# Values and gates of the last 64 tokens in plain float32, in two 64-column tiles side by side

## The chip, the cores and the metric

The kernel runs on one core of a Trainium2 chip. The metric is the device time of one execution in microseconds (us). The core has five engines that each run their own instructions in a fixed order and wait for each other by semaphores: PE (TensorE, matrix products), DVE (VectorE), ACT (ScalarE), POOL (GpSimd) and SP (SyncE, which here issues most of the transfers, the DMAs). Instructions are put in order when the kernel is built.

## The reference

Three stages follow one another: linear attention with a normalised output, a channel mixing stage, and an attention with four experts of which each token takes two. The change concerns the third stage. For each of 8 batches with 576 tokens of 512 features (here `x`, the output of the stage before):

```python
logits = x @ w_gate                      # 4 experts
topk = np.argpartition(-logits, K, axis=-1)[..., :K]     # K = 2
...
w = np.exp(sel)
w /= w.sum(-1, keepdims=True) + 1e-09
for e in range(E):
    q = x @ wq[e]                        # 64 columns each
    k = x @ wk[e]
    v = x @ wv[e]
    scores = scale * (q @ k.transpose(0, 2, 1))
    scores = np.where(causal, -1000000000.0, scores)
    ...
    a = np.exp(scores)
    a /= a.sum(-1, keepdims=True) + 1e-09
    ye = a @ v @ wo[e]
    # out += (gate weight of e, for tokens that chose e) * ye
```

`x` is the product of two arrays that the stage before leaves in memory, `x2d` and `sgd` (a gate).

## The kernel before

`phase_a` and `phase_v` compute the first two stages, `phase2` the experts. Most products are not done in plain float32 but from two parts: a value is split (`split`, L70 to L72) into a rounded part (`...h`, made by ACT) and the rest (`...l`, made by DVE or POOL), and `mm3` (L74 to L78) issues three matmuls for each block of 128 rows of the contraction. The contraction over 512 features has four blocks (KD), so one product of this kind has 12 matmuls. In the trace their lines are L76, L77 and L78.

The weights of `phase2` are loaded and split by `weights2` and its `load_w` during `phase_v`. The value weights of four experts (4 x 64 columns) and the gate weights (4 columns) lie side by side, 260 columns, as `wgh` and `wgl`. The unsplit weights pass through a staging tile `wst` with two buffers.

In `phase2` the 576 tokens of a batch lie in five chunks: four of 128 and a last one of 64. They are also cut into halves [0, 256) and [256, 576).

- `prep(b, hf)` loads a half of the two arrays (tiles `x2in` and `gin`, L779, issued by SP), multiplies them on POOL (L786), and splits the product into `x2h` (ACT, L787) and `x2l` (POOL, L788). `x2in` has two buffers, so a half of the next batch takes the buffer of the same half of this batch.
- `qk_group` makes queries or keys of a pair of experts for a half: 12 matmuls that move 256 or 320 columns. For a second half it also copies the last 64 queries into the block-diagonal tile `bd` (POOL, L821).
- `v_group(b, c)` makes values and gates of a chunk: 12 matmuls that move 260 columns, with the tokens as the stationary side, and a copy to `vs` (DVE, L831). For the last chunk (c = 4) it multiplies the last 128 tokens and copies only rows 64 to 127; rows 0 to 63 of that chunk of `vs` are zeroed once. Then `gate` (DVE, one exponential on ACT) turns the logits of the whole batch into gate weights `wg` and `wl`.
- `scores` computes scores of a chunk of queries for a pair of experts (matmuls of 64 x 128 tiles, L902), or for the last chunk of both experts at once from `bd` (L887). `expo` takes the exponential (ACT, L914), `norm` multiplies it by the inverse sum and the gate weight (POOL, L931), `transp` transposes it (PE, L951) four steps later, `attnv` multiplies it by the values in plain float32, with the two experts of a pair in two tiles of 64 columns (L978), and `wo_group` applies the output weights; its result goes out by a DMA of SP (L1005).

Scores of the last chunk for the first pair need a probability tile `pr` of 576 columns, of which the last transpose takes 128 columns in two blocks.

A batch has 18 steps (`seq`). Lists (`fill_q`, `fill_o`, `fill_n`, spread over the steps) say which group is issued at which step: the key, value and gate groups of the next batch run during this batch, and `v_group(b, 4)` is the last of them. The scheduler of the build may still move an instruction against others on its engine by its own estimate of when its data is there. On PE, `v_group(b, 4)` ends up between `v_group(b, 3)` and the first scores of batch b.

## Time and profile before

| | us |
|---|---|
| median of 3 runs (978.44 to 979.56) | 978.5 |
| the profiled execution | 979.24 |
| its span in the trace | 977.5 |
| PE busy in the span | 944.1 (97%) |
| DVE busy | 635.1 (65%) |
| ACT busy | 538.2 (55%) |
| POOL busy | 382.5 (39%) |

The profile shows one execution. The span runs from the first to the last recorded instruction, so the whole execution is 1.74 us longer than it. Shares are an average over the three stages. In `phase2`, which fills the span from about 600 us on, one batch takes 46.1 us. In a row of the timeline, "x12" is a run of twelve like instructions, the first figure is when the run starts and the second how long it lasts until its last end; the ends of matmuls are modelled, so the distance from start to start says more than the duration of one. A plain float32 matmul leaves two records.

### The profile page before, as it was taken

To read this page: it belongs to the slowest core of one execution; us is meant where nothing else is said; L and a number is where in the kernel's file an instruction comes from. 1 tells how busy PE (TensorE), PEld (TensorE's weight loads), DVE (VectorE), ACT (ScalarE), POOL (GpSimd) and SP (SyncE) were. 2 spreads that over 40 slices of the span, in tenths; PEclk is the share of its full clock that TensorE was granted. 3 is DMA by queue.
4 is the path that set the end of the run, shared out by engine and by line. 5 is a ranking of instruction groups with operands and counts; after the bars stand their busy time and mean duration, and the time that the engine had idled before them with its cause. 6 is when DMAs were issued, how large, how long until landed. Compare 5 with 4: busy or idle time off the path is not lost.

```text
span 977.5 us, 20974 instructions
## 1 busy us (share of the span) xinstructions
PE 944.1 (97%) x7912; PEld 866.8 (89%) x7912; DVE 635.1 (65%) x1535; ACT 538.2 (55%) x1320; POOL 382.5 (39%) x510
## 2 busy tenths in 40 slices
PE   5779999999999999999999999999999999999998
PEld 2668899999999999999999999888988888888977
DVE  4897675867595855458888873666556556556553
ACT  4664766656565665445454544546364646455554
POOL 0035052424252512632222225757373736364331
PEclk9789999999999999999999999999999999999999
DMA  9752637363736222766454545223131404020102
GB/s 340 239 164 92 224 107 240 107 222 99 233 111 210 95 80 92 214 196 195 155 157 159 157 135 186 79 77 103 44 120 28 121 26 146 2 98 1 50 13 85
DMA packets 81108, 127.19 MB, mean 130 GB/s; under 512 B 6512, under 2 KB 65392, under 8 KB 81008
## 3 DMA queue, kind: packets, MB, share of 16 engines
q1 hardware_dynamic: 71360, 112.36, 35.7%
q10 hardware_dynamic: 9648, 13.51, 4.2%
q8 instruction: 62, 1.02, 0.5%
q14 instruction: 38, 0.31, 0.1%
HBM read 78.66 MB, written 47.19 MB: 129 GB/s over the span
## 4 chain that ended last, share of the span: by engine, by line
PE 82%; DVE 7%; ACT 5%; DMA 3%; issue 2%; POOL 1%; ACTq 0%; SPq 0%; POOLq 0%; DVEq 0%
PE acc L76 16%; PE acc L77 16%; PE acc L78 15%; PE qa L676 7%; PE acc L978 5%; PE qd L676 4%; PE pt L951 4%; PE acc L676 4%; PE s L902 3%; PE acc L296 2%; PE s L887 1%; PE po L312 1%; PE acc L66 1%; ACT pr L914 1%; DMA kkd<-ksq 1%
## 5 line engine op out<-in xcount | busy, mean ns | idle before, releaser
L433 POOL TENSOR_TENSOR ksq<-rl 128x288 f32<-128x288 f32 x128 | 101.9, 803 | 150.1 <-ACT rl L431 144.9
L77 PE MATMUL acc<-mixl,wkh 128*128 128x288 f32 x512 | 154.1, 302 | 0.4 <-DVE mixl L66 0.4
L76 PE MATMUL acc<-mixh,wkh 128*128 128x288 f32 x512 | 151.1, 299 | 3.4 <-ACT mixh L405 2.8
L78 PE MATMUL acc<-mixh,wkl 128*128 128x288 f32 x512 | 151.2, 296 | 0.0
L914 ACT ACTIVATE pr<-pr,nm 128x256 f32<-128x256 f32 (+4 forms) x144 | 83.5, 581 | 72.1 <-DVE nm L868 71.3
L931 POOL TENSOR_SCALAR pr<-pr,rc,wg 128x512 f32<-128x512 f32 (+3 forms) x128 | 76.3, 609 | 72.5 <-DVE wg L861 54.2
L76 PEld LDWEIGHTS acc<-mixh,wkh 128*128 128x128 f32 x512 | 96.4, 190 | 4.6 <-ACT mixh L405 3.3
L77 PEld LDWEIGHTS acc<-mixl,wkh 128*128 128x128 f32 x512 | 97.0, 189 | 2.4 <-DVE mixl L66 0.6
L78 PEld LDWEIGHTS acc<-mixh,wkl 128*128 128x128 f32 x512 | 97.3, 190 | 0.0
L399 DVE TENSOR_TENSOR mixl<-xm,mixh 128x288 fp32r<-128x288 f32 x116 | 58.3, 538 | 51.7 <-ACT mixh L405 51.7
L431 ACT ACTIVATE rl<-acc 128x288 f32<-128x288 f32 x128 | 51.7, 406 | 71.0 <-PE acc L78 52.6
L868 DVE CUSTOM_DVE_ANT_0 pr<-s,mask 128x256 f32<-128x256 f32 (+4 forms) x144 | 66.9, 481 | 21.6 <-PE pt L951 16.9
L76 PE MATMUL acc<-mixh,wrh 128*128 128x288 f32 x240 | 74.6, 311 | 0.9 <-ACT sg L66 0.9
L404 DVE SCALAR_TENSOR_TENSOR xm<-xT,pars,xm 128x288 f32<-128x288 f32 x116 | 68.9, 623 | 5.1 <-ACT xm L396 5.0
L396 ACT ACTIVATE xm<-xT,nus 128x288 f32<-128x288 f32 x120 | 61.0, 533 | 18.7 <-DVE mixl L399 8.8
L78 PE MATMUL acc<-mixh,wrl 128*128 128x288 f32 x240 | 71.0, 296 | 0.0
L77 PE MATMUL acc<-mixl,wrh 128*128 128x288 f32 x240 | 70.4, 293 | 0.0
L76 PE MATMUL acc<-x2h,wqh 128*128 128x256 f32 (+1 forms) x224 | 69.5, 310 | 0.0
L72 DVE TENSOR_TENSOR kk<-tv,kk 128x1152 fp32r<-128x1152 f32 x32 | 51.4, 1607 | 27.2 <-ACT kk L71 27.1
L77 PE MATMUL acc<-x2l,wqh 128*128 128x256 f32 (+1 forms) x224 | 66.1, 295 | 0.0
L78 PE MATMUL acc<-x2h,wql 128*128 128x256 f32 (+1 forms) x224 | 66.1, 295 | 0.0
L951 PE MATMUL pt<-ident,pr 128*128 128x128 f32 x400 | 63.4, 277 | 0.6
(252 smaller groups left out, 2732.4 us busy)
## 6 DMA issues: line engine op xcount, KB each, us to landing
kkd<-ksq SPq DMA_DIRECT2D x128, 144.0 KB, 1.8
kin<-kkd SPq DMA_DIRECT2D x32, 576.0 KB, 4.1
kvt<-in_kv SPq DMA_DIRECT2D x24, 512.0 KB, 5.7
qt<-in_qT SPq DMA_DIRECT2D x16, 576.0 KB, 6.8
x2d<-vo SPq DMA_DIRECT2D x16, 576.0 KB, 3.7
sgd<-sg ACTq DMA_DIRECT2D x56, 144.0 KB, 3.2
out<-ob SPq DMA_DIRECT2D x28, 288.0 KB, 2.3
x2in<-x2d SPq DMA_DIRECT2D x7, 640.0 KB, 5.2
```

Source lines behind the costliest of these rows:

```text
L76: ten.matmul(ps, wh(i), xh(i), start=(i == 0), stop=False)
L77: ten.matmul(ps, wh(i), xl(i), start=False, stop=False)
L78: ten.matmul(ps, wl(i), xh(i), start=False, stop=(i == n - 1))
L396: act.activation(xs[p], xT[:, p, h * HS:(h + 1) * HS], AF.Copy, scale=nu[:, p:p + 1])
L399: vec.tensor_sub(xl[:, p, :], xs[p], xh[:, p, :].bitcast(F32))
L404: vec.scalar_tensor_tensor(xs[p], xT[:, p, cols(h)], mu[:, p:p + 1], xs[p], op0=ALU.mult, op1=ALU.add)
L433: nc.gpsimd.tensor_mul(sq, rl, rl)
L676: nc.tensor.matmul(q[:, :HS], a[:, i, ms_], c[:, i, :], start=(start and i == 0 and n == 0), stop=(stop and i == KH - 1 and n == 2), skip_ ...
L868: nc.vector.tensor_tensor_reduce(out=pr[:R, k0:k0 + kn], in0=s[:R, :kn], in1=mk, scale=1.0, scalar=lo, op0=ALU.add, op1=ALU.min, accum_out ...
L914: nc.scalar.activation(pr[:, :L], pr[:, :L], AF.Exp, bias=nm, scale=-1.0, accum_out=sms[b, p, j][:, e2:e2 + 1])
L931: nc.gpsimd.tensor_scalar(pr[:, :L], pr[:, :L], rc[:, r:r + 1], wg, op0=ALU.mult, op1=ALU.mult)
L951: nc.tensor.transpose(pt[:, (i - i0) * P:(i - i0 + 1) * P], pr[:, k1 - P:k1], ident)
```

## The change

`load_w` can be given the tile to load into, and the value and gate weights are loaded into a new tile `wg_raw` that stays. They are still split for the other chunks. For the last chunk, `v_group` takes the 64 tokens unsplit as the stationary side, from `xf`, and `wg_raw` as the moving side, in plain float32: for each of the four blocks one matmul of 128 columns (experts 0 and 1) whose result lies in rows 0 to 63, and one of 132 columns (experts 2 and 3, and the gates) whose result lies in rows 64 to 127. Two copies bring them to `vs`. Which rows of `vs` are zeroed changes with this, and the last chunk of the first pair takes a tile `wide` of its own that is 64 columns longer, zero there, so that the last transpose reads 128 columns that match the new rows. For batch 0, `xf` is a small tile that two more ACT copies fill at the end of `phase_v`; for the others it is `x2in` itself.

```diff
-        def load_w(wh, wl, w, kt, f, scaled=0):
-            st = w2.tile([P, DM], F32, name="wst", bufs=2)
+        wg_raw = W["wg_raw"] = w2.tile([P, KD, NV + E], F32, name="wg_raw")
+
+        def load_w(wh, wl, w, kt, f, scaled=0, st=None):
+            if st is None:
+                st = w2.tile([P, DM], F32, name="wst", bufs=2)
...
-            load_w(wgh, wgl, w_vg, i, NV + E)
+            load_w(wgh, wgl, w_vg, i, NV + E, st=wg_raw[:, i, :])
...
+                        if n > 2:
+                            act.activation(W["xf"][:, 2 * n - 6:2 * n - 4, :], x[:, :, x.shape[2] - MN:], AF.Copy)
...
+                xf[b] = x2[:, :, :w]
...
+            wide = sb.tile([P, S + P - MN], F32, name="wide", bufs=1)
+            nc.gpsimd.memset(wide[:, S:], 0.0)
+            xf = {0: W["xf"]}
...
-                    nc.gpsimd.memset(st_[b]["vs"][:P - MN, NC - 1, :], 0.0)
+                    nc.gpsimd.memset(st_[b]["vs"][MN:, NC - 1, :VC], 0.0)
+                    nc.gpsimd.memset(st_[b]["vs"][:P - MN, NC - 1, VC:], 0.0)
...
-                nc.vector.tensor_copy(t["vs"][P - n:, c, :], acc[P - n:, :NV + E])
-                if c == NC - 1:
+                if c < NC - 1:
+                    mm3(acc[:, :NV + E], lambda i: xh[:, i, a:a + P], lambda i: xl[:, i, a:a + P], lambda i: wgh[:, i, :], lambda i: wgl[:, i, :], KD)
+                    nc.vector.tensor_copy(t["vs"][:, c, :], acc[:, :NV + E])
+                else:
+                    parts = [(slice(0, MN), slice(0, VC)), (slice(P - MN, P), slice(VC, NV + E))]
+                    for i in range(KD):
+                        for rs, cs in parts:
+                            nc.tensor.matmul(acc[rs, :cs.stop - cs.start], xf[b][:, i, -MN:], W["wg_raw"][:, i, cs], start=(i == 0),
+                                             stop=(i == KD - 1), skip_group_check=True)
+                    for rs, cs in parts:
+                        nc.vector.tensor_copy(t["vs"][rs, c, cs], acc[rs, :cs.stop - cs.start])
                     gate(t["vs"][:, :, NV:], t["wg"])
...
-                pr = sb.tile([P, S], F32, name="pr", bufs=6)
+                pr = wide if j == NC - 1 and p == 0 else sb.tile([P, S], F32, name="pr", bufs=6)
...
-                        k1 = CH[i][0] + CH[i][1]
+                        k1 = CH[i][0] + (P if p == 0 else CH[i][1])
```

The order of instructions moves with it at three places, which recur with each batch. In the rows below a name with a number is one buffer or one array (`x2d_60` and `sgd_76` belong to one batch, `x2d_61` and `sgd_77` to the next), and "waits" lists the engines and DMA queues whose semaphores an instruction waits for.

On SP, before: the transfers of a batch in the middle of `phase2`.

```order
L779 DMA x2in<-x2d_60 128x4x256 [waits DMAHW5_49,Pool_49]
L1005 DMA out<-ob 128x576 [waits Activation_49] x2
L779 DMA gin<-sgd_77 128x4x256 [waits DMAHW6_49,Pool_49]
L1005 DMA out<-ob 128x576 [waits Activation_49]
L779 DMA x2in<-x2d_60 128x4x320 [waits DMAHW7_49,Pool_49]
L1005 DMA out<-ob 128x576 [waits Activation_49]
L779 DMA gin<-sgd_77 128x4x320 [waits DMAHW0_49,Pool_49]
```

On SP, with the change, the same transfers.

```order
L785 DMA x2in<-x2d_60 128x4x256 [waits DMAHW5_49,Pool_49]
L1026 DMA out<-ob 128x576 [waits Activation_49] x2
L785 DMA gin<-sgd_77 128x4x256 [waits DMAHW6_49,Pool_49]
L1026 DMA out<-ob 128x576 [waits Activation_49] x2
L785 DMA x2in<-x2d_60 128x4x320 [waits DMAHW7_49,PE_49]
L785 DMA gin<-sgd_77 128x4x320 [waits DMAHW0_49,Pool_49]
```

The load of the second half of `x2in` moves behind the last `out` transfer, and waits for PE (the last chunk's product of the batch that holds the buffer) where it waited for POOL.

On POOL, before: from the last norms of one batch to the first norms of the next.

```order
L931 TENSOR_SCALAR pr<-pr,rc,wg 128x512 x2
L786 TENSOR_TENSOR x2in<-x2in,gin 128x320 x4
L931 TENSOR_SCALAR pr<-pr,rc,wl 128x576
L821 COPY bd_7814<-qs 64x2x64 x2
L931 TENSOR_SCALAR pr<-pr,rc,wg 128x128 x2
L931 TENSOR_SCALAR pr<-pr,rc,wg 128x256 x2
L931 TENSOR_SCALAR pr<-pr,rc,wg 128x384 x2
```

On POOL, with the change, the same stretch.

```order
L952 TENSOR_SCALAR pr<-pr,rc,wg 128x512 x2
L952 TENSOR_SCALAR pr<-pr,rc,wl 128x576
L834 COPY bd_7814<-qs 64x2x64 x2
L793 TENSOR_TENSOR x2in<-x2in,gin 128x320 x4
L952 TENSOR_SCALAR pr<-pr,rc,wg 128x128 x2
L952 TENSOR_SCALAR pr<-pr,rc,wg 128x256 x2
L952 TENSOR_SCALAR pr<-pr,rc,wg 128x384 x2
```

The multiply of the second half moves behind the last chunk's norm and the `bd` copies, directly ahead of the first norms (128 x 128) of the next batch.

On PE, before: the first transposes, scores and value products that follow the query groups after `v_group(b, 4)`.

```order
L951 MATMUL pt<-ident,pr 128x128 x4
L902 MATMUL s<-ks,qs 128x128 x6
L902 MATMUL s<-ks,qs 128x256 x6
L978 MATMUL acc<-pt_9817,vs 64x320 x6
L978 MATMUL acc<-pt_9817,vs 64x192 x2
L978 MATMUL acc<-pt_9817,vs 64x64 x2
L951 MATMUL pt<-ident,pr 128x128 x3
L978 MATMUL acc<-pt_9664,vs 64x256 x2
L978 MATMUL acc<-pt_9664,vs 64x128 x2
L887 MATMUL s<-ks,bd_7814 128x288 x3
L951 MATMUL pt<-ident,pr 128x128 x7
```

On PE, with the change, the same stretch; two transposes that stood singly among the query groups stand at its head.

```order
L972 MATMUL pt<-ident,pr 128x128 x2
L999 MATMUL acc<-pt_9811,vs 64x320 x6
L999 MATMUL acc<-pt_9811,vs 64x192 x2
L999 MATMUL acc<-pt_9811,vs 64x64 x2
L972 MATMUL pt<-ident,pr 128x128 x4
L923 MATMUL s<-ks,qs 128x128 x6
L923 MATMUL s<-ks,qs 128x256 x4
L908 MATMUL s<-ks,bd_7814 128x288 x3
L923 MATMUL s<-ks,qs 128x256 x2
L999 MATMUL acc<-pt_9658,vs 64x256 x2
L999 MATMUL acc<-pt_9658,vs 64x128 x2
L972 MATMUL pt<-ident,pr 128x128 x6
```

The scores (64 x 128 tiles) move behind the first value product and are cut in two by the scores from `bd`, so that PE passes seven times from one tile shape to another where it passed five times.

## Rows read from the trace of the kernel before

**Rows 1.** First part of the page: busy time, share and instructions of each engine.

```profile
PE 944.1 (97%) x7912; PEld 866.8 (89%) x7912; DVE 635.1 (65%) x1535; ACT 538.2 (55%) x1320; POOL 382.5 (39%) x510
```

**Rows 2.** Windows: one batch of `phase2`; stretch, length, busy time, clock, DMA.

```profile
736.00:782.00 46.00, 45.73 (x374) 40.51 (x370) 27.17 (x101) 24.38 (x75) 24.86 (x39) 1.00 0.26 78
```

**Rows 3.** Timeline of PE, `v_group` of the last chunk: start, length, instruction.

```profile
744.70 0.28 PE L76 MATMUL acc<-wgh,x2h 128*128 128x260 f32 x1
...
746.04 0.28 PE L78 MATMUL acc<-wgh,x2l 128*128 128x260 f32 x1
746.26 1.49 PE L902 MATMUL s<-ks,qs 64*128 64x384 f32 x12
```

**Rows 4.** Timeline of PE at 709 us: scores, value products, transposes.

```profile
709.47 0.96 PE L902 MATMUL s<-ks,qs 64*128 64x128 f32 x12
710.36 2.28 PE L978 MATMUL acc<-pt,vs 128*64 128x320 f32 x20
712.57 0.55 PE L951 MATMUL pt<-ident,pr 128*128 128x128 f32 x3
713.04 0.87 PE L978 MATMUL acc<-pt,vs 128*64 128x256 f32 x8
713.84 0.67 PE L887 MATMUL s<-ks,bd 128*128 128x288 f32 x3
```

**Rows 5.** Timeline of PE at 666 us, where the same scores stand in two pieces.

```profile
665.85 0.72 PE L902 MATMUL s<-ks,qs 64*128 64x128 f32 x8
666.50 0.41 PE L887 MATMUL s<-ks,bd 128*128 128x288 f32 x1
...
668.37 0.50 PE L902 MATMUL s<-ks,qs 64*128 64x256 f32 x4
668.80 0.55 PE L951 MATMUL pt<-ident,pr 128*128 128x128 f32 x3
```

**Rows 6.** Timeline of PE at 751 us: a single transpose and the query groups.

```profile
751.01 0.30 PE L951 MATMUL pt<-ident,pr 128*128 128x128 f32 x1
751.18 0.41 PE L76 MATMUL acc<-x2h,wqh 128*128 128x320 f32 x1
751.43 0.31 PE L77 MATMUL acc<-x2l,wqh 128*128 128x320 f32 x1
...
752.61 0.31 PE L76 MATMUL acc<-x2h,wqh 128*128 128x320 f32 x1
```

**Rows 7.** Timeline of SP's queue at 771 us: transfers issued.

```profile
770.54 0.33 SPq L1005 DMA_DIRECT2D out<-ob  x1
771.10 0.53 SPq L779 DMA_DIRECT2D x2in<-x2d  x1
```

**Rows 8.** Timeline of POOL, 744 to 782 us: norms and the multiply.

```profile
750.48 3.23 POOL L931 TENSOR_SCALAR pr<-pr,rc,wg 128x128 f32<-128x128 f32 x6 [7.67 <-DVE wg L861]
...
769.36 0.87 POOL L931 TENSOR_SCALAR pr<-pr,rc,wg 128x128 f32<-128x128 f32 x2
...
776.60 3.38 POOL L786 TENSOR_TENSOR x2in<-x2in,gin 128x320 f32<-128x320 f32 x4
```

**Rows 9.** DMA issues, whole span: size, median us from issue to landing.

```profile
x2in<-x2d SPq DMA_DIRECT2D x7, 640.0 KB, 5.2
gin<-sgd SPq DMA_DIRECT2D x7, 640.0 KB, 4.3
```

**Rows 10.** DMA issues between 832 and 880 us alone.

```profile
x2in<-x2d SPq DMA_DIRECT2D x1, 640.0 KB, 4.6
```

**Rows 11.** Waits of PE, 420 to 470 us: total, times, longest us.

```profile
PE qa L676 <- DVE vo L687: 1.8, 2, 1.2
```

**Rows 12.** Timeline of DVE at 440 us: splits of the value weights.

```profile
440.12 3.27 DVE L72 TENSOR_TENSOR wgl<-wst,wgh 128x260 fp32r<-128x260 f32 x2 [0.18 <-ACT wgh L71]
```

**Rows 13.** Groups by line, 690 to 978 us: the last chunk's copy, weight loads of L978.

```profile
L978 PEld LDWEIGHTS acc<-pt,vs 128*64 128x64 f32 x371 | 24.4, 136 | 16.2 <-issue 1.4 <-ACT pt L960 1.1
...
L831 DVE COPY vs<-acc 64x260 f32<-64x260 f32 x6 | 2.6, 431 | 6.2 <-PE acc L78 6.2
```

More of the change, by code (lines that the diff above doesn't have):

```diff
@@ L738, in phase_v @@
                     W["x2t"] = [[x2p.tile([P, KD, c1 - c0], F32R, name=f"x2{i}{u}") for u in "hl"] for i, (c0, c1) in enumerate(cuts)]
+                    W["xf"] = x2p.tile([P, KD, MN], F32, name="xf")
                     parts = []
@@ L795, in phase2 @@
                     nc.gpsimd.memset(bd[i][p].bitcast(F32), 0.0)
+            VC = NPR * D
+            wide = sb.tile([P, S + P - MN], F32, name="wide", bufs=1)
+            nc.gpsimd.memset(wide[:, S:], 0.0)
+            xf = {0: W["xf"]}
             def batch(b):
@@ L829, in v_group @@
                 acc = ps.tile([P, HW], F32, name="acc", bufs=AB)
-                mm3(acc[:, :NV + E], lambda i: xh[:, i, a:a + P], lambda i: xl[:, i, a:a + P], lambda i: wgh[:, i, :], lambda i: wgl[:, i, :], KD)
-                nc.vector.tensor_copy(t["vs"][P - n:, c, :], acc[P - n:, :NV + E])
-                if c == NC - 1:
+                if c < NC - 1:
[9 more added lines that the diff above has]
+                        nc.vector.tensor_copy(t["vs"][rs, c, cs], acc[rs, :cs.stop - cs.start])
                     gate(t["vs"][:, :, NV:], t["wg"])
```

## The prediction

> **What bounds the kernel now.** I read the busy shares first: PE works through 97% of the span [rows 1]. One batch of the expert stage, seen in the windows, says the same of the stage that the change edits: 45.7 of 46.0 us of PE, at full granted clock, while no other engine passes 27.2 [rows 2]. So what counts is how long PE's own list is, and whether PE now waits where it did not. I went to the timelines of PE, SP and POOL next, around the last chunk's product and around what the change moves.
>
> The profiled execution took 979.24 us, 0.74 above the median. The terms are differences from that execution and I add them to the median, 978.5; counted from the profiled time itself the result stands 0.74 higher. A difference under 0.2% (1.96 us, so bounds at 976.54 and 980.46) can't be told from no change here.
>
> **The product itself: gain 0.41 us a batch.** The old one occupies PE from 744.70 to the start of the scores at 746.26, 1.56 us [rows 3]. The new one exists in the trace only by its nearest kin, the value products, also plain float32 into two tiles of 64 columns. Ten calls of one of them (20 records) move, if the two tiles of a pair run side by side, 2 passes of 3 x 320 + 192 + 64 columns, 2432, and take 712.57 - 710.36 = 2.21 us; the other moves 2 x (256 + 128) = 768 in 713.84 - 713.04 = 0.80 [rows 4]. The slope is 1.41 us / 1664 = 0.85 ns a column, with 0.15 us beside it for entering and leaving. The new product has four pairs, the longer partner 132 columns: 2 x 4 x 132 = 1056 columns, 0.90 + 0.15 = 1.05 us. The old product leaves its full tile once anyway: its last step takes 0.22 where its steps take 0.12 (1.34 us from first to last start, 11 steps) [rows 3]. The new one is entered from a full tile as well, so I add 0.10: 1.15, a gain of 0.41.
>
> A rule of the Trainium skill speaks against this: "TensorE: Matmul & The Clock Gate", Part 3 (Packing small matmuls), says that a weight load runs beside a matmul in flight only when the two lie in different groups of rows, and two column tiles share all 128 rows. By it each load would stand in the open. The trace disagrees: the product of 0.80 us has eight records and a weight load for each, and eight loads of 0.136 [rows 13] are 1.09 alone. By the rule the sixteen loads of the new product would add 2.18 us to it, eight times over, and the time would be 997 (rival D); by the rows they add nothing.
>
> **The order of PE after it: loss 0.35.** The product is followed by the same scores as before, but further on two more passages from one tile shape to another stand in each batch (seven for five). One passage is bounded by the same scores in one piece and in two: 710.36 - 709.47 = 0.89 us [rows 4] against 0.65 + 0.43 = 1.08 [rows 5], so 0.19; the 0.15 above is the lower value. Two cost 0.30 to 0.38, taken as 0.35. In return no transpose stands singly among the query groups any more: there the transpose took 0.17 and the re-entry 0.25 for a step of 0.15 (1.18 / 8) [rows 6], against 0.16 for one among three [rows 4]. That gives back about 0.1 (0 to 0.16).
>
> **The held buffer: loss about 0.45.** This is the term that decides. For batches after the first the product reads `x2in` itself, so the buffer of the second half is free only when the product is done. Its load, which SP issued at 771.10 [rows 7], some 20 us ahead of the next batch's product, now waits for PE. For batches 2 to 7, six times, it starts at what I call T0, the end of the product (746.26 in the old rows). On POOL the multiply that needs it stands directly ahead of the next batch's first norms, and PE's first two transposes need these. So the chain is: 0.1 for the wait and issue, the transfer, the multiply 3.38, two norms 0.87 [rows 8], and 0.1 to PE (the two tenths are estimates; SP's queue and PE's 0.10 passages show such sizes). The transfer's price is known only from other company: 5.2 us median in the old place beside out transfers, 4.6 in one batch [rows 9, 10], and 4.3 for `gin`, of the same size [rows 9]. In the new place the out transfers have been issued long before, and only `gin` follows, which itself waits for the multiply; so I lean to the low end and take 4.4. Then the transposes can start at T0 + 0.1 + 4.4 + 3.38 + 0.87 + 0.1 = T0 + 8.85. PE gets there when scores and first query groups are through, which was at 751.01, T0 + 4.75 [rows 6], and 24 query matmuls more, 0.10 + 24 x 0.1475 = 3.64: T0 + 8.39. The wait is 0.45, and 1.25 with 5.2 for the transfer. With 4.0 it would still be some 0.05; PE's list behind the transposes gives nothing to cover it, since a value product waits for them, and the scores that used to cover stand behind that.
>
> Queued on SP behind the held load are `gin` and the first half of the following batch; both are wanted later than this multiply, and cost nothing of their own. The same goes for the splits to `x2h` and `x2l`: their query groups come at the end of the batch. POOL stands idle or waits during the transfer; before, its first norms began at 750.48 when the gates were there [rows 8], that is T0 + 4.2, so the multiply, at T0 + 4.6, takes the place in which norms ran.
>
> **What costs nothing.** A second DVE copy lies on the way to the gates: the old one takes 0.43 [rows 13], two smaller ones perhaps 0.15 more than one and at most 0.43. The gates were there at T0 + 4.2; the norms wait for the multiply until T0 + 7.9, so 3 us of cover stand over it. If the held load were no delay, the cover would still be PE's 8.39 less 4.2 less 0.87. The two memsets run once for each of two buffers. The longer tile `wide` is exchanged for one of six and changes no length. The two small ACT copies stand at the end of the stage before, each of 128 columns; by the 0.43 of 260 columns on DVE they are 0.9 us together at the very most, beside PE's last products there.
>
> **The loading of the weights: loss 0.3, between -1.5 and +2.** At 420 to 470 us PE waits twice for DVE's result of L687, 1.8 us in all, 1.2 the longest [rows 11]. Beside it the splits of the value weights are slow on DVE, 3.27 us for two [rows 12]. With `wg_raw` the loads no longer wait for a free staging tile, so the splits move ahead, and those of the output weights move to where they were. That may take the waits away (-1.5) or shift them and lengthen one (+2). The load is the same, so I take a little over nothing.
>
> **The sum.** A batch in which the load is held: -0.41 + 0.35 - 0.1 + 0.45 = +0.29, six times +1.7. The first batch's product gains 0.41; the last batch's, which is followed by a full tile and so pays one more passage, 0.25. With +0.3 for the weights: 1.7 - 0.66 + 0.3 = +1.4. 978.5 + 1.4 = 979.9.
>
> **The rivals.**
>
> A, the forecast: a small wait, a transfer of 4.3 to 4.8 us. Per batch +0.2 to +0.7, with the weights' term from -0.5 to +0.8: 978.4 to 982.0, likeliest 979.9. Chance 0.48; 0.40 of it within 0.2%, 0.08 slower.
>
> B, slower: the transfer lands as late as the median of its old rows, 5.2 us. It decides from about 4.5 on, where the sum passes the 0.2%. Wait 1.25, per batch +1.09, six times 6.5, less 0.36 as above: +6.2, 984.7. For it: that is the median of seven old transfers, and a delayed norm delays everything behind it on POOL. Against it: out transfers shared the queues in these. Chance 0.29.
>
> C, faster: PE doesn't wait, because the transfer alone is quicker than any row (4.0 or less). Per batch -0.16, six times -1.0, with -0.66 and +0.3: 977.2. If also the two extra passages cost nothing, since PE's later transposes wait for POOL in either order, -0.51 per batch: 975.1. Centre 976.1. Chance 0.20; 0.17 faster, 0.03 within 0.2%.
>
> D, the product doesn't do what it says: the two column tiles run one after the other. 0.90 more, 2.05 us for 1.56 [rows 3]; eight times that more than A is 987.1, and with the sixteen weight loads in the open instead 979.9 + 8 x 2.18 = 997.3. The value products speak against both. Chance 0.03 together.
>
> **How the numbers follow.** Faster 0.17 from C; same 0.40 + 0.03; slower 0.08 + 0.29 + 0.03. The likeliest case gives 979.9, with its own range 978.4 to 982.0. The full range takes in A, most of C down to 975.2 and the half of B up to 985.0.
>
> **What would show it.** On PE's timeline the new product should stand for 1.0 to 1.2 us up to the scores, sixteen records of which pairs start together; 2 us mean D. On SP's queue, the 640 KB load of `x2in` should start within 0.2 us of the product's end and land 4.3 to 4.8 us later; the multiply on POOL follows at once and the 128 x 128 norms behind it. The waits of PE should then name POOL's norm (L952 there) for the first transposes with some 0.3 to 0.7 us, six times; over 1 us is B, none is C. Around 440 us the waits for L687 should add up to between 0.3 and 3.8 us. I am wrong altogether if PE's first wait of a batch is for something else, for instance for scores or their exponentials, or if PE's batches differ in length by more than these terms.

## The result and the profile after

The changed kernel takes 985.15 us (median of 6 executions, 984.81 to 986.07) against 978.75 for the kernel before beside it: a ratio of 1.0062, 95% interval 1.0051 to 1.0073. It is slower by 6.4 us. The profiled execution took 984.81 us with a span of 983.0. The likeliest case of the prediction (no difference, 979.9) did not come true. The time lies 0.15 us above the range, which ends at 985.0; as a ratio to the 978.5 that the prediction starts from (978.5 x 1.0062 = 984.6) it lies just inside. Either way it stands near the end that rival B gave the range, but by another mechanism than B's.

Of the shares on the page little moves, as in [rows 1]: PE has the same work in a longer span.

```profile
PE 943.2 (96%) x7944; PEld 862.8 (88%) x7944; DVE 643.9 (66%) x1543; ACT 539.0 (55%) x1322; POOL 383.5 (39%) x519
```

A batch shows it. The distance from the first scores behind one last-chunk product to the next is 792.39 - 746.26 = 46.13 us before (the start of the last row in [rows 3]) and 794.38 - 747.20 = 47.18 after. The rows are of PE's timeline, one of before and then three of after, in which the new product and the scores behind it stand.

```profile
792.39 0.79 PE L902 MATMUL s<-ks,qs 64*128 64x384 f32 x6
```

```profile
746.15 1.12 PE L850 MATMUL acc<-wg_raw,x2in 128*64 128x128 f32 x16
747.20 1.49 PE L923 MATMUL s<-ks,qs 64*128 64x384 f32 x12
...
794.38 0.79 PE L923 MATMUL s<-ks,qs 64*128 64x384 f32 x6
```

The new product takes 747.20 - 746.15 = 1.05 us, half a microsecond less than the old one. Over the five batches between 700 and 940 us the distances add up to 240.49 us for 234.55, a loss of 5.9 us; everything else together is 0.4 us shorter. So the time is lost inside the batches, and the view of PE's waits, here from 690 to 935 us, says where: total, times, longest, of waits of 0.15 us or more. Before, this stretch had one wait of 0.2 us. Without these waits the four batches from 700 to 890 us are as long as before, 45.9 us for 46.0.

```profile
PE pt L972 <- DVE pt L983: 4.4, 5, 1.1
PE acc L76 <- DVE qs L72: 1.5, 4, 1.0
```

First the head of the batch, where the prediction looked. The load of the held buffer is issued on SP, as foretold, 0.1 us after the product's end, and the median landing of this transfer is 4.3 us (second row, the view of DMA issues from 690 to 975 us; 4.4 had been taken).

```profile
747.30 0.53 SPq L785 DMA_DIRECT2D x2in<-x2d  x1
```

```profile
x2in<-x2d SPq DMA_DIRECT2D x5, 640.0 KB, 4.3
```

POOL's timeline shows the multiply behind it and the norms behind that, and then an unbroken run of work:

```profile
751.75 3.38 POOL L793 TENSOR_TENSOR x2in<-x2in,gin 128x320 f32<-128x320 f32 x4 [7.58 <-PE acc L78]
755.12 3.23 POOL L952 TENSOR_SCALAR pr<-pr,rc,wg 128x128 f32<-128x128 f32 x6
...
763.11 1.70 POOL L795 TENSOR_TENSOR x2l<-x2in,x2h 128x320 fp32r<-128x320 f32 x2
764.80 0.81 POOL L952 TENSOR_SCALAR wide<-wide,rc,wl 128x576 f32<-128x576 f32 x1
765.59 1.56 POOL L795 TENSOR_TENSOR x2l<-x2in,x2h 128x256 fp32r<-128x256 f32 x2
767.49 0.88 POOL L952 TENSOR_SCALAR pr<-pr,rc,wg 128x128 f32<-128x128 f32 x2 [0.33 <-DVE sm L945]
```

On PE the first two transposes start at 755.90, 8.70 us after the product (8.85 had been worked out). PE has lost 0.3 us there at most: 0.15 before the second query group and 0.16 beyond the 8.39 + 0.15 at which it could have been there. At the transposes themselves the view names no wait.

```profile
752.27 0.42 PE L76 MATMUL acc<-x2h,wqh 128*128 128x320 f32 x1 [0.15 <-DVE qs L72]
...
755.90 0.47 PE L972 MATMUL pt<-ident,pr 128*128 128x128 f32 x2
```

In one of the five batches the second query group waited 1.00 us instead. There POOL's multiply began at 704.40, while DVE was at two small copies that take 0.34 us in the batch at 751.42, and the query split of DVE stands behind these. DVE first, then PE:

```profile
704.25 1.04 DVE L856 COPY wl<-wg 64x2 f32<-64x2 f32 x2
```

```profile
705.80 0.41 PE L76 MATMUL acc<-x2h,wqh 128*128 128x320 f32 x1 [1.00 <-DVE qs L72]
```

The large wait comes eleven microseconds later, at the transposes of the long tile `wide`, in each of the six batches with a held load (0.55 to 1.09 us):

```profile
766.30 0.60 PE L972 MATMUL pt<-ident,pr 128*128 128x128 f32 x4
766.90 0.30 PE L972 MATMUL pt<-ident,wide 128*128 128x128 f32 x1
768.29 0.55 PE L972 MATMUL pt<-ident,wide 128*128 128x128 f32 x3 [1.09 <-DVE pt L983]
```

There are two PSUM buffers for transposes. The block of four in the last row needs the one that DVE has to empty of the four at 766.30. DVE's timeline says why that was late:

```profile
764.75 2.43 DVE L945 TENSOR_SCALAR sm<-sm 128x2 f32<-128x2 f32 x1
767.21 0.17 DVE L947 RECIPROCAL rc<-sm 128x2 f32<-128x2 f32 x1
...
767.56 0.67 DVE L983 COPY pt<-pt 128x512 f32<-128x512 f32 x1
```

An addition to two numbers in each partition, which takes 0.15 to 0.17 us where POOL is idle, takes 2.43. It ends at 767.18, when POOL's unbroken run (763.11 to 767.15) ends. The same place before: the addition took 0.62 us, and the copy followed it at once.

```profile
764.16 0.62 DVE L924 TENSOR_SCALAR sm<-sm 128x2 f32<-128x2 f32 x1 [1.11 <-ACT pr L914]
764.69 0.68 DVE L962 COPY pt<-pt 128x512 f32<-128x512 f32 x1
```

In the kernel before POOL had a split directly behind the norm, too (764.72), and yet the addition got in: it ended with the norm, at 764.78. So work without a gap on POOL does not always keep it out. The six batches of the changed kernel differ in this as well, and the last column is e2 below, the same order of PE (but for two rows) without the addition:

| wait at | PE's wait, us | addition ahead of the copy, us | wait in e2, us |
|---|---|---|---|
| 673.79 | 0.91 | 2.18 | 0.55 |
| 721.11 | 0.55 | 0.41 | 0.56 |
| 768.29 | 1.09 | 2.43 | 0.56 |
| 815.58 | 1.09 | 2.42 | 0.53 |
| 862.58 | 0.85 | 0.90 | 0.56 |
| 909.49 | 0.82 | 0.87 | 0.54 |
| sum | 5.3 | | 3.3 |

POOL has no more to do in a batch than before (24.96 us for 24.86), but the multiply of the second half has moved from the end of the batch, where POOL was idle, to its head. In 26 us from the first of this work on, POOL is busy for 24.39, where it was 20.11 (windows; the columns are stretch, length, busy time of PE, PE loads, DVE, ACT and POOL, clock, DMA share and GB/s; first after, then before).

```profile
751.70:778.20 26.50, 25.26 (x196) 21.60 (x195) 17.72 (x57) 17.49 (x53) 24.39 (x38) 1.00 0.34 106
```

```profile
750.40:776.60 26.20, 26.02 (x206) 22.79 (x205) 15.96 (x57) 17.52 (x53) 20.11 (x33) 1.00 0.36 111
```

### The profile page after: what moved, and what is told of

It reads as the page before. It is cut to its first block, busy times and chain, and to the rows that moved or that the text cites. A ratio compares the mean times of both kernels' runs of the same rounds, so it can differ in the third digit from the quotient of the medians.

```text
span 983.0 us, 21096 instructions
## 1 busy us (share of the span) xinstructions
PE 943.2 (96%) x7944; PEld 862.8 (88%) x7944; DVE 643.9 (66%) x1543; ACT 539.0 (55%) x1322; POOL 383.5 (39%) x519
## 4 chain that ended last, share of the span: by engine, by line
PE 81%; DVE 10%; ACT 3%; issue 2%; DMA 2%; POOL 1%; ACTq 0%; SPq 0%; DVEq 0%; POOLq 0%
PE acc L76 15%; PE acc L77 15%; PE acc L78 14%; PE qa L679 7%; PE acc L999 5%; PE pt L972 5%; PE qd L679 4%; PE acc L679 4%; PE s L923 3%; PE acc L66 2%; PE acc L299 2%; PE po L315 1%; PE s L908 1%; DVE pr L889 1%; DVE sm L945 1%
## 5 line engine op out<-in xcount | busy, mean ns | idle before, releaser
L935 ACT ACTIVATE pr<-pr,nm 128x128 f32<-128x128 f32 (+4 forms) x136 | 77.2, 568 | 68.4 <-DVE nm L889 66.4
L889 DVE CUSTOM_DVE_ANT_0 pr<-s,mask 128x128 f32<-128x128 f32 (+4 forms) x136 | 63.8, 484 | 26.2 <-PE pt L972 21.4
L793 POOL TENSOR_TENSOR x2in<-x2in,gin 128x256 f32<-128x256 f32 (+1 forms) x56 | 43.4, 806 | 56.6 <-PE acc L78 38.1
```

Of the source, the lines that this page charges most:

```text
L889: nc.vector.tensor_tensor_reduce(out=pr[:R, k0:k0 + kn], in0=s[:R, :kn], in1=mk, scale=1.0, scalar=lo, op0=ALU.add, op1=ALU.min, accum_out ...
L935: nc.scalar.activation(pr[:, :L], pr[:, :L], AF.Exp, bias=nm, scale=-1.0, accum_out=sms[b, p, j][:, e2:e2 + 1])
```

## The experiments

The theory after the result: the hold puts 3.4 us of POOL's work at the head of the batch; POOL then works without gaps, shuts DVE's additions out, and PE waits for copies behind them. ("Shut out" is short for an addition that lasts longer than elsewhere and ends when an instruction of POOL ends.) Against it stands that the new order of PE alone, with the transposes of the last chunk close behind four others, is too dense for two PSUM buffers. The table gives, for each kernel, its median and the ratio to the kernel before on the same chip, the mean distance from batch to batch (four batches, 700 to 890 us, of the profiled execution), and PE's waits with a name from 690 to 935 us. The ratio need not be exactly that of the two medians.

| kernel | us | ratio, 95% interval | batch | PE's named waits |
|---|---|---|---|---|
| before | 978.75 | 1 | 46.07 | 0.2 |
| after | 985.15 | 1.0062 (1.0051 to 1.0073) | 47.20 | 5.9 |
| e1_free_buffer | 989.78 | 1.0114 (1.0101 to 1.0127) | 47.44 | 6.9 |
| e2_no_sum_add | 982.26 | 1.0045 (1.0030 to 1.0059) | 46.58 | 2.8 |
| e3_hold_only | 983.51 | 1.0044 (1.0031 to 1.0057) | 46.28 | 0 |
| e4_copy_xf | 982.10 | 1.0043 (1.0027 to 1.0059) | 46.27 | 4.9 |
| e5_no_add_swap | 984.65 | 1.0058 (1.0046 to 1.0071) | 47.21 | 4.1 |
| e6_copy_no_add | 977.40 | 0.9986 (0.9977 to 0.9995) | 45.65 | 0.2 |
| e7_before_no_add | 976.88 | 0.9982 (0.9973 to 0.9991) | 45.85 | 0.7 |
| e8_raw_weights | 979.84 | 1.0008 (0.9999 to 1.0017) | 45.93 | 0.2 |
| e9_multiply_on_dve | 1004.21 | 1.0245 (1.0222 to 1.0268) | 49.47 | 14.7 |
| e10_dve_no_add_swap | 1002.16 | 1.0224 (1.0203 to 1.0245) | 50.62 | 14.4 |
| e11_copy_own_load | 977.64 | 0.9976 (0.9962 to 0.9989) | 45.75 | 0 |
| e12_split_on_dve | 988.15 | 1.0088 (1.0074 to 1.0101) | 47.38 | 4.5 |

**A second buffer (e1).**

```diff
-                x2, g = [sb.tile([P, KD, HW], F32, name=name, bufs=2) for name in ("x2in", "gin")]
+                x2 = sb.tile([P, KD, w], F32, name=f"x2in{hf}", bufs=1 + hf)
+                g = sb.tile([P, KD, HW], F32, name="gin", bufs=2)
```

> The changed kernel, with a second buffer for the second half of x2in, so that its load no longer waits for the last chunk's product of the batch before but is issued a batch earlier. The order of instructions stays nearly that of the changed kernel (the multiply still stands ahead of the first norms on POOL; 87 of 5,179 rows of PE differ). Theory of the held buffer: the late multiply pushes POOL's norms and splits back, and everything that PE waits for later in the batch (0.6 to 1.1 us at the transposes of the long tile, 0.15 to 1.0 at the query group) follows from it. Then these waits, 6.7 us in six batches, go for the most part: 979 to 981 us. Rival, the order: PE's transposes of the last chunk stand too close together for two PSUM buffers, whoever is late on POOL. Then the waits stay at 0.5 us or more a batch: 983 to 985 us.

Measured: 989.78, a miss, and no test of the hold. The build used the second buffer to load one batch further ahead, at the same place: the load is still issued 0.1 us after a product (799.50), and POOL's multiply still begins 4.58 us after it, ahead of the norms. The rows are of SP's and of POOL's timeline.

```profile
799.60 0.53 SPq L786 DMA_DIRECT2D x2in<-x2d  x1
```

```profile
804.08 3.37 POOL L794 TENSOR_TENSOR x2in<-x2in,gin 128x320 f32<-128x320 f32 x4 [7.60 <-PE acc L78]
```

The batches are therefore those of the changed kernel, with the same addition of 2.43 us and the same wait of 1.09. Its span is 5.0 us longer than the changed kernel's: 1.8 of these lie before the expert stage and 2.4 in the first batch, where PE waits 1.5 us for a norm at 627.50; the rest was not followed up.

**Without the addition (e2).**

```diff
-                nc.vector.tensor_scalar(sm, sm, 1e-9, None, op0=ALU.add)
```

> The changed kernel without the addition of 1e-9 to the sums of the softmax (left out of the computation), a DVE instruction on 128 x 2 elements that took 2.43 us in one place behind which PE's transposes waited 1.09 us. PE's order stays the same but for 2 rows. Theory of DVE being shut out while POOL works through its backlog: the buffer copy behind that instruction comes about 0.7 us earlier, so the wait at the transposes of the long tile falls from 0.6 to 1.1 us to 0.4 or less: 981 to 983 us. Rival, the copy is late for another reason (its place in DVE's order, or the transposes being too dense): the wait stays within 0.2 us and the time at 984 to 985.5.

Measured: 982.26, as the theory has it. With PE's order unchanged but for two rows, batches shorten by 0.6 us on average (0.2 of it is the one wait of 1.00 us at 705.80, which is 0.14 here), and the wait in front of the long tile's block falls to 0.53. What is left of it is the density: DVE is idle and waits for the four transposes, copies them in 0.69, and PE waits for that. First PE, then DVE:

```profile
812.52 0.60 PE L971 MATMUL pt<-ident,pr 128*128 128x128 f32 x4
813.07 0.30 PE L971 MATMUL pt<-ident,wide 128*128 128x128 f32 x1
813.90 0.55 PE L971 MATMUL pt<-ident,wide 128*128 128x128 f32 x3 [0.53 <-DVE pt L982]
```

```profile
813.15 0.69 DVE L982 COPY pt<-pt 128x512 f32<-128x512 f32 x1 [0.51 <-PE pt L971]
```

So of the 1.09 us in this batch, DVE's being shut out is a half and PE's denser order the other. Over the six batches (the table above) 3.3 of the 5.3 us stay without the addition: the denser order is the larger share, the addition 2.0 us.

The whole times do not show even that share. Leaving the addition out takes 0.0017 off the ratio of the changed kernel and, in e7 below, 0.0018 off that of the kernel before; without it the change costs as much as with it (1.0045 to 0.9982), as far as intervals of 0.001 to 0.0015 to either side can tell. The batches differ, 0.62 us shorter here and 0.22 there. In e7's profiled execution 1.8 of 2.8 us are gained ahead of 653 us, in front of all batches with a held load, and it was not followed whether they belong to the addition.

**The hold alone (e3).**

```diff
                 x2t[b, hf] = (xh, xl)
+                xf[b] = x2[:, :, :w]
...
+                if c == NC - 1 and b > 0:
+                    nc.tensor.matmul(acc[:, NV + E:NV + E + 4], xf[b][:, 0, -P:], ident[:, :4], start=True, stop=True, skip_group_check=True)
```

> The kernel before, with only the hold: one small extra matmul (4 columns, its result unused) on the unsplit tile in the last chunk's product, so that the load of the next second half waits for PE as in the changed kernel. The product stays in its old form, no tile shape changes. On POOL the multiply moves ahead of the first norms, as in the changed kernel. Theory of the held buffer: about 1.0 to 1.4 us a batch lost in five or six batches, 984 to 987 us. Rival, the loss comes from the new product, its tile shapes and the order after it: 979 to 980.5 us.

Measured: 983.51, ratio 1.0044; between the two expectations. In the profiled execution 1.4 us of it lie before the expert stage, where the two kernels do the same, so they are no effect of the hold. The batches of the hold alone are 0.2 us longer, not 1.0 to 1.4, with no wait that the view names: the scores are cut in two there as well. POOL is as late as in the changed kernel, but PE's order, made for the old product, sets other work between the transposes. And POOL works without a gap here as well, from 811.94 to 822.15, yet the additions get in between its instructions, as this one does between a norm and two splits (DVE, then POOL):

```profile
813.02 0.62 DVE L929 TENSOR_SCALAR sm<-sm 128x2 f32<-128x2 f32 x1 [1.13 <-ACT pr L919]
```

```profile
812.79 0.83 POOL L936 TENSOR_SCALAR pr<-pr,rc,wl 128x576 f32<-128x576 f32 x1
813.58 1.71 POOL L789 TENSOR_TENSOR x2l<-x2in,x2h 128x320 fp32r<-128x320 f32 x2
```

Of the rest of the difference, 1.1 us lie in the batch from 654 to 703, the first with a held load, and 1.1 behind 888 us; they were not followed. So in these four batches the hold alone costs 0.2 us each, less than the 0.35 and 0.45 that the prediction had for order and wait; the wait at the last chunk's transposes doesn't come with the hold alone.

**No hold (e4).**

```diff
-                xf[b] = x2[:, :, :w]
...
+                    if hf == 1:
+                        if i == 0:
+                            xf[b] = sb.tile([P, KD, MN], F32, name="xfb", bufs=2)
+                        tc.keep_in_program_order(nc.scalar.activation(xf[b][:, i, :], x[:, w - MN:], AF.Copy))
```

> The changed kernel, with the last 64 tokens of each batch copied by ACT into a small tile of their own (four copies of 64 columns a batch), as the changed kernel does for batch 0 alone, so that the buffer is never held. The scheduler then puts POOL's multiply back behind the norms of 512, as before. Theory of the held buffer: what is left is the gain of the product, 0.4 us in each of eight batches, less up to 0.35 us of tile shapes where the new order keeps them: 975.5 to 978.5 us. Rival, product and tile shapes cost the time: 982 us or more.

Measured: 982.10, as the rival had it, but not for the rival's reason. With the multiply back at its old place, PE's order is a third one, and PE waits at two places of each batch for copies of DVE. At the first, four transposes follow six others with six scores between them. At the second, twelve matmuls of an output product stand between two blocks of four, but the copy of the first block stands behind an addition that POOL shuts out for 1.73 us, in each of the five batches (PE, then DVE):

```profile
808.66 0.63 PE L976 MATMUL pt<-ident,pr 128*128 128x128 f32 x4 [0.39 <-DVE pt L987]
...
813.07 0.66 PE L976 MATMUL pt<-ident,wide 128*128 128x128 f32 x4 [0.57 <-DVE pt L987]
```

```profile
810.49 1.73 DVE L949 TENSOR_SCALAR sm<-sm 128x2 f32<-128x2 f32 x1 [0.43 <-ACT pr L939]
```

So a kernel without the hold loses time at the same spot. The hold is one way into it, not the only one.

**Without the addition, blocks swapped (e5)**, e2's edit and this one.

```diff
-                blocks = [(0, j + 1)] if n == P else [(j, 1), (0, j)]
+                blocks = [(0, j + 1)] if n == P else [(0, j), (j, 1)]
```

> The changed kernel without the addition of 1e-9 (left out, as in the second run), and with the two blocks of the last chunk's transposes in the other order: the block of four first, then the single one. In the second run PE still waited 0.53 us a batch in front of the block of four, for the PSUM buffer that DVE was copying from the four transposes just before. Theory that PE's new order is too dense for two PSUM buffers: the block of four now takes the buffer that ACT has emptied earlier, the single one the late buffer, with 0.44 us of transposes between: the wait falls to 0.1, six times 0.4 less than the second run's 982.3: 979.5 to 980.5 us. Rival, DVE is late for its own reasons by more than that: the wait moves to the single transpose and the time stays at 981.5 to 982.5.

Measured: 984.65, a miss. The wait for PSUM went as expected (0.19), but the time it gave did not stay: PE came earlier to the second pair's transposes and waited there for POOL's norms, which were late (PE, then POOL).

```profile
816.56 0.33 PE L971 MATMUL pt<-ident,wide 128*128 128x128 f32 x1 [0.19 <-DVE pt L982]
822.87 0.55 PE L971 MATMUL pt<-ident,pr 128*128 128x128 f32 x3 [0.61 <-POOL pr L951]
```

```profile
819.33 2.84 POOL L793 TENSOR_TENSOR x2in<-x2in,gin 128x256 f32<-128x256 f32 x4 [0.48 <-POOL pr L951]
822.15 2.81 POOL L951 TENSOR_SCALAR pr<-pr,rc,wg 128x384 f32<-128x384 f32 x4
```

Here the multiply of the next first half stands ahead of the norms that PE wants. POOL is no longer behind with its work: it has stood idle for 0.48 us ahead of that multiply, whose transfer SP had issued at 815.27, behind the held load and its `gin`. What PE waits for in this stretch is set by POOL's order, with one instruction queued behind another one's wait.

**No hold and no addition (e6)**, the edits of e4 and e2 together.

> The fourth run's kernel (last 64 tokens copied by ACT, no buffer held) without the addition of 1e-9 (left out of the computation). The scheduler now sets other work between the four-block transposes of the last chunk and those ahead of them. In the fourth run PE waited 0.4 and 0.6 us a batch there for DVE's copies, once behind an addition that took 1.73 us. Theory that the loss is made of these waits: batches of 45.4 us instead of 46.3, 976 to 978 us, faster than the kernel before. Rival, the product's tile shapes and the copies cost the time: 981 to 982 us.

Measured: 977.40, as the theory had it: batches of 45.65 us and no wait at the last chunk. PE's order is another one than in e4, so the run does not say whether the order or the missing addition took the waits away. And e7 belongs beside it.

**The kernel before without the addition (e7)**, the edit of e2.

> The kernel before without the addition of 1e-9 (left out of the computation). Its trace shows additions of 0.6 to 0.9 us too, but PE waited only some 0.2 us a batch for DVE. Theory that the addition hurts only where PE waits for a copy behind it: 977.5 to 979 us. Rival, it is a cost of its own in either kernel, as large as in the changed one (2.9 us): 975 to 976 us.

Measured: 976.88, a little below the theory's range: the addition costs the kernel before 0.2 us a batch too, though the view named hardly a wait. Both e6 and e7 beat the two given kernels, and against each other they can't be told apart. The batches with the new product are 0.2 us shorter (45.65 for 45.85), and that is given back outside them. The addition can go without harm by this argument: each row's largest exponential is 1, so its sum is at least 1, which 1e-9 does not change in float32.

**The weights' loading alone (e8)**, the first two blocks of the change's diff.

> The kernel before, with only the loading of the value weights changed: into a tile of their own that no other load waits for, from which they are split as before; the products are the old ones. PE's order differs in 13 of 5,201 rows. The prediction's term for this was +0.3 us, between -1.5 and +2: 977 to 980.5 us. If PE's waits around 440 us (1.8 us) go, 977; if the splits lengthen one of them, up to 980.5.

Measured: 979.84, ratio 1.0008, an interval that contains no change. PE's waits from 420 to 470 us are 4.1 us for 1.8 [rows 11]:

```profile
PE qd L679 <- ACT vq L684: 2.7, 2, 1.5
PE qa L679 <- DVE vo L690: 1.4, 1, 1.4
```

**The multiply on DVE (e9).**

```diff
-                    nc.gpsimd.tensor_mul(x, x, g[:, i, :w])
+                    (nc.vector if hf else nc.gpsimd).tensor_mul(x, x, g[:, i, :w])
```

> The changed kernel, with the multiply of the second half (four instructions a batch, 3.38 us on POOL) done by DVE. PE's order is the changed kernel's, row for row, and the load still waits for the product; only POOL no longer has the multiply ahead of its norms. Theory of POOL's backlog: with the multiply at the head of the batch, POOL works without a gap from 4.6 us after the product on, DVE's additions are shut out behind it and its norms are late; without it the additions take 1 us or less and the wait in front of the long tile's transposes falls from 1.09 to about 0.5: 980.5 to 982.5 us. Rival, PE's order alone (transposes too dense for two PSUM buffers): PE's waits stay within 0.2 us a batch and the time at 984 to 985.5. DVE gets 1.8 us more work a batch, which may cost some of the gain.

Measured: 1004.21, a miss in the sum. I had priced DVE's extra work and forgotten its queue: now DVE stands still until the held transfer lands, with the query splits behind it, and PE waits 2.3 to 2.5 us a batch for these. At the place in question the theory's number came out, 0.56 for 1.09 at the same order of PE (0.53 to 0.56 in all five batches), and no addition takes more than 0.63 us:

```profile
809.85 0.41 PE L76 MATMUL acc<-x2h,wqh 128*128 128x320 f32 x1 [2.48 <-DVE qs L72]
825.16 0.55 PE L972 MATMUL pt<-ident,wide 128*128 128x128 f32 x3 [0.56 <-DVE pt L983]
```

**The same with e5's edits (e10)**, the edits of e9, e2 and e5 together.

> The fifth run's kernel (no addition of 1e-9, which is left out; block of four transposes first) with the multiply of the second half on DVE as well; PE's order is the fifth run's, row for row. There the wait for PSUM was gone (0.2 us) and PE waited 0.6 to 0.8 us for POOL's norms of 384 instead. Theory of POOL's backlog: that wait goes too, and batches take about 46.2 us instead of 47.2: 978.5 to 980 us, which is the prediction's sum without its wait (-0.41 + 0.35 - 0.1). Rival, another wait takes its place once more: 983 us or above.

Measured: 1002.16, the same miss for the same reason (11.7 us of waits for the query splits from 690 to 935 us); it says nothing on what it was made for.

**e6 with a load of their own for the raw weights (e11).**

```diff
-            load_w(wgh, wgl, w_vg, i, NV + E, st=wg_raw[:, i, :])
+            load_w(wgh, wgl, w_vg, i, NV + E)
...
+        for i in range(KD):
+            nc.sync.dma_start(wg_raw[:, i, :], w_vg[i * P:(i + 1) * P, :])
```

> The sixth run's kernel (tokens copied, no hold, no addition), with the raw weights brought by a load of their own at the end of the weights, and the split weights staged as in the kernel before. If the earlier splits in the stage before cost the 1 us that the eighth run measured (979.84 against 978.71), this takes it back: 976 to 977 us, faster than the sixth run's 977.4 and no slower than the seventh's 976.9. If that 1 us is scatter between executions, 977 to 978.

Measured: 977.64, ratio 0.9976; its interval overlaps those of e6 and e7. What the loading of the weights costs is below what these runs can tell.

**First-half splits on DVE (e12).**

```diff
-                    nc.gpsimd.tensor_sub(xl[:, i, :], x, xh[:, i, :].bitcast(F32))
+                    (nc.gpsimd if hf else nc.vector).tensor_sub(xl[:, i, :], x, xh[:, i, :].bitcast(F32))
```

> The changed kernel, with the four splits of the first half (x2l, 0.73 us each on POOL, 2.9 us a batch) done by DVE. The load still waits for the product, the multiply stays on POOL ahead of the first norms, and PE's order is the changed kernel's but for 6 of 5,179 rows. Nothing on DVE waits for the held transfer this time, as it did in the ninth run. Theory of POOL's unbroken run: POOL no longer has two splits (1.56 us) between the long tile's norm and the next ones, so DVE's addition gets in about 1 us earlier, the wait in front of the long tile's block of transposes falls from 1.09 to about 0.5, and batches take 46.6 us instead of 47.2: 981 to 982.5 us. Rival, PE's order alone: waits and batches stay within 0.2 us, 984 to 986; DVE's additional 1.7 us a batch could make it slower.

Measured: 988.15, a miss in the sum once more. With the two splits gone from POOL's list the addition takes 0.32 for 2.43 us and PE's wait falls to 0.55, as expected, although POOL's next instruction again follows without a gap. But two additions later, POOL's multiply begins 0.05 us ahead of one and holds it for all its four instructions, 2.78 us. DVE first, then POOL:

```profile
813.50 0.32 DVE L945 TENSOR_SCALAR sm<-sm 128x2 f32<-128x2 f32 x1
...
817.43 2.78 DVE L945 TENSOR_SCALAR sm<-sm 128x2 f32<-128x2 f32 x1 [0.78 <-ACT pr L935]
```

```profile
817.38 2.79 POOL L793 TENSOR_TENSOR x2in<-x2in,gin 128x256 f32<-128x256 f32 x4
```

The norm behind that addition is late, and PE waits 1.22 us at 820.94 for it, so this batch is 1.2 us longer than in the changed kernel (48.5 for 47.3). The batch from 653 to 701 us is like it: an addition of 2.77 us, a wait of 1.20, 48.5 us for 47.3. The three others have neither and take 46.95 to 47.05 us, on average 0.2 less than in the changed kernel, where 0.6 less had been expected. In two of these three the same addition meets the same four multiplies and gets in behind the first of them (0.73 us at 770.34, 0.72 at 865.88).

## Why the prediction was right and wrong

**The product.** Right: a column at the rate of the value products, pairs side by side. It was sized at 1.15 us with 0.10 for entering and took 1.05, so it gains 0.51 instead of 0.41. The weight loads lie beside the matmuls, as [rows 4] said: sixteen of 0.136 us are 2.18, twice the whole product. D fell.

**The tile shapes.** A batch has 16 passages where it had 13: the two that I had found in the stretch behind the product, and the product's own, priced there with 0.10. The size is about right: apart from waits, PE's steps grow by 0.35 us a batch in the scores and by 0.4 in the transposes, and shrink by 0.2 in the query and key groups. With the gain of the product that comes to about nothing, where the sum without its wait had -0.16.

**The held buffer.** The chain was right link by link: issue 0.1, landing 4.3 for 4.4, multiply 3.38, first transposes 8.70 us after the product for 8.85. PE lost 0.3 us there for 0.45, in one batch 1.0. But the signs that I had named did not come: PE's waits name no norm of POOL at the first transposes, and the first named wait of a batch is for DVE's query split, which I had called being wrong altogether. Rival B's transfer of 5.2 us did not come; that its price, 984.7, lies near the measured 985.15 is chance.

**The steps that failed** are two terms that the sum has at nothing. The larger is in the order of PE. I had read it only up to the second value product and priced passages alone; further down, four transposes of another tile now stood directly ahead of the long tile's, too dense for two PSUM buffers. That is a wait of 0.55 us in each of six batches, 3.3 us (e2). The smaller is the sentence that the splits behind the held load, like the transfers, "cost nothing of their own". Rival B says that a delayed norm delays everything behind it on POOL, but I priced only the first thing that PE waits for. The multiply is 3.38 us more in a stretch in which POOL had some 6 us free (20.11 of 26.20). POOL's runs closed up, some of DVE's short additions stood behind them for 0.9 to 2.4 us, copies of PSUM stood behind the additions, and the wait grew to 0.82 to 1.09 us in five of the six batches: 2.0 us more. Together that is the missing 5 us, eleven microseconds behind the place that I had looked at.

Shown are: that the batches are longer by PE's named waits (45.9 us for 46.0 without them); that 0.53 to 0.56 us of each stay when the additions are left out (e2) or are short (e9, e12, and the batch at 721.11 of the changed kernel itself); and that time freed there can go to another instruction in the same queues (e5, and two batches of e12). Not shown is why an addition is held over one instruction of POOL in one place and over four in another: work without a gap on POOL is not enough (e3). The whole times of e2 and e7 don't confirm the share of the additions. Also not shown is a kernel with the hold in which POOL is not late: none of the edits kept the hold without making another engine wait.

**The weights.** 0.3 between -1.5 and +2; e8 gives 0.8 with an interval from -0.1 to 1.7, and the changed kernel reached the expert stage 0.24 us earlier. In the changed kernel PE's waits from 420 to 470 us add up to 2.7, 1.7 of them for the line that was L687, inside the 0.3 to 3.8 given as a sign. Inside the bounds, then; the size stays open.

**What was hidden** stayed hidden: the two copies to `vs` take 0.29 us each, and the gates were not waited for, but the copies behind the gates met the multiply once (704.25).

**A sum.** Rival A's own terms (+0.2 to +0.7 six times, -0.66, and -0.5 to +0.8) give 978.5 to 982.8, not 978.4 to 982.0; it changes nothing above.

## What to carry to other kernels

An engine that is idle on average can set the time of a stretch: when a wait moves work of that engine from where it was idle to where it is needed, count its free time in that stretch, not in the span, and follow the delay through every queue until it is absorbed. When an instruction is placed behind a new wait, everything behind it on its engine waits too; moving the work to another engine (e9) moves the wait into that queue. And a change whose gain is half a microsecond a batch can be lost to the order that a build makes of it, so read the changed order for the whole batch and not only around the edit.

## What the runs showed of the hardware

DVE and POOL are not independent. DVE's addition of a constant to 128 x 2 numbers takes 0.15 to 0.17 us when POOL is idle and up to 2.78 when it is not, and a long one ends when an instruction of POOL ends, within 0.04 us in the rows above. The Trainium skill says, in "SBUF — State Buffer", section "SBUF: two separate sides", that DVE operations of some kinds (in a two-port mode, or with two inputs in SBUF) and GpSimd operations share a pair of ports as an exclusive lock that whoever starts first holds "for the whole instruction". The rows agree that DVE waits for the end of an instruction of POOL, and at times go further: the 2.43 us spanned the end of one POOL instruction and three more, and the 2.78 us all four of a multiply. At other times DVE got its turn between two that followed without a gap: 0.62 us before and in e3, 0.72 behind the first of four in e12. What decides is not shown. Two copies of 64 x 2 numbers within SBUF were caught once as well, 1.04 us for 0.34. Reciprocals of the same sums took 0.13 to 0.17 us throughout, POOL busy or not, and copies of 128 x 512 numbers out of PSUM 0.64 to 0.69.

Leaving the additions out was worth 1.8 us to the kernel before (e7; by its interval 0.9 to 2.6), although its view of waits named almost nothing to gain. A delay of this kind sits inside the DVE instruction's own duration, so DVE's idle time does not show it; where PE's list got shorter was not followed.
